# A spectral mixing layer and a state-space convolution in one kernel: the planner counts the wait for VectorE's own result, and the first tiles are split in another order

## The chip, the core and the metric

The kernel runs on one core of a Trainium2 chip. The metric is the device time of one execution in microseconds (us). A core has engines with instruction streams of their own: TensorE (PE in the profile; its weight loads are PEld), VectorE (DVE), ScalarE (ACT), GpSimd (POOL) and SyncE (SP, which here issues nearly all the transfers). They meet only at semaphores, and each runs its stream in the order in which it was written.

## The reference

Two independent parts, whose results stand side by side in the output:

```python
# A: x is (2048, 512); the four DFT matrices are inputs
a = x @ dft_hid_re.T;  b = x @ dft_hid_im.T
ya = dft_seq_re @ a - dft_seq_im @ b
# B: u is (2048, 512); A, C are (512, 128) complex; dt is (512,)
P = exp((A * dt)[:, :, None] * arange(2048))        # (512, 128, 2048)
K = 2 * real(einsum("dn,dnl->dl", C * dt, P))       # taps of a convolution, per channel
yb = irfft(rfft(u, 4096) * rfft(K, 4096))[:2048] + u * D_skip
out = concatenate([ya, yb])                          # (2048, 1024), float32
```

## The kernel before, in words

**Part A (class Fnet)** is dense matmul. Each float32 tile of 128x512 is split into a high and a low part: ScalarE copies it to `hi` (line 181), VectorE subtracts to get `lo` (line 183). One step of a product is then three matmuls, hi·hi, lo·hi and hi·lo (line 294), called a *triple* here; one moving tile feeds four triples. There are 12 groups (8 against x, 4 against the hidden-dimension matrix) and 640 triples in all. Three split moving tiles are held at once (`DEPTH`), four raw ones (`RAWS`).

**Part B (class Ssm)** makes the convolution's taps from tables of powers. The 512 channels go in 16 chunks of 32. For each chunk two tables grow by doubling, each step a product (`mul`, line 524, into `prod`) and the sum of its halves (`add`, line 533, into `t`): table 1 (`tables1`, 12 VectorE steps; two buffers `t1`) holds the coarse powers, table 2 (`tables2`, 19 steps; a single buffer `t2`) the fine ones, where even entries come from a squaring on ScalarE (lines 540, 547, 553). In `order`'s rows below both are called `t`: `t_124` is table 2, another number is table 1 of one chunk. A step of a table reads what the step ahead of it has written. When both tables of a chunk are done, TensorE makes the chunk's *taps* with 64 small matmuls (`taps`, line 720). They free both tables, so table 2 of the next chunk starts only after them. Then come an FFT as small matmuls (lines 793 for u, 750 for the taps, 871), the product of the spectra on VectorE (`product`, lines 887, 889, 897, 900) and the inverse (lines 907, 954). From the last chunk's taps on, no table work is left.

**What sets the order.** Nothing is moved by the compiler: `Plan` is a small list scheduler that runs when the program is written, and its choices become the order of every engine's stream. Each process is a generator; it yields the engine and an estimated duration, and waits for events and for counts of free buffers (`Sem`). Of the processes that are ready, the one that can start earliest is written next, and of those that can start equally early the one of lower urgency number (`key`, line 122). Where a process goes from one engine to another, `HOP` (0.3 us) is added to the time from which its next step is ready; between two steps on the same engine nothing is. Table 2 has urgency 2, table 1 2.2, part B's other work 1, and part A's matmuls 5, so that triples fill what part B leaves of TensorE. A tile's split has urgency 3 while three split tiles are ahead of TensorE, else 0.

**The start.** `load_x0` brings in the first 128 columns of x tile 0 and splits them, so that the first quarter of the first triples can begin; `load_x1` brings in the rest of tile 0 and the other x tiles; `load` the moving tiles, the first of them through ScalarE's queue. `warm` runs three matmuls on zeros ahead of them. A count `slots` of four raw x buffers holds the loads back.

Of the kernel before, what the change touches and what calls it, by code (L numbers as in the profile page):

```python
# [46 lines left out]
    return [np.ascontiguousarray(a.astype(np.float32)) for a in (f1u, f1k, w2, ia, ib)]  # L47


HOP, LATENCY = 0.3, 3.3  # L50
STREAM = 5


class Sem:
# [11 lines left out]
class Plan:  # L66
# [11 lines left out]
    def step(self, p, value):  # L78
        self.now = p[0]
        while True:  # L80
            try:
                r = p[3].send(value)
            except StopIteration:
                return
            value = None
            if isinstance(r, Event):
                if r.time is None:
                    r.waiting.append(p)
                    return
                p[0] = max(p[0], r.time)  # L90
            elif isinstance(r, Sem):
                if not r.free:
                    r.waiting.append(p)
                    return
                p[0] = max(p[0], r.free.pop(0))
            else:
                if r[0] != p[5]:
                    p[0] += HOP
                p[4], p[5] = r, r[0]
                self.ready.append(p)  # L100
                return
            self.now = p[0]
# [18 lines left out]

    def key(self, p):
        engine, _, *urgency = p[4]
        return max(p[0], self.free.get(engine, 0.0)), urgency[0]() if urgency else p[1], p[2]

    def run(self):

        while self.ready:
# [4 lines left out]
            if engine == "pe":  # L133
                stream = p[1] >= STREAM
                if stream != self.streaming:
# [7 lines left out]
def act(cols):  # L143
    return 0.09 + cols * 0.00085


def dve(cols, rate=1.0):
    return (62 + cols / rate) / 960


def load(kb):
    return max(0.55, kb / 330)


class Fnet:
# [36 lines left out]
    def warm(self):  # L192

        z, ps = self.pool.tile([128, DM], F32, name="y", bufs=STAGED), self.psum.tile([128, DM], F32, name="acc")
        yield "dve", 0.3
        self.nc.vector.memset(z, 0.0)
        yield "pe", 2.2
        for n in range(3):
            self.nc.tensor.matmul(ps[:, :216], z[:, :128], z[:, 256:472], start=n == 0, stop=n == 2)

    def still(self, k):
        return [self.pool.tile([128, DM], F32R, name=f"x_{m}{k}") for m in ("hi", "lo")]
# [17 lines left out]
                                     op=OP.subtract)  # L220
        self.plan.set(self.x0_ev)

    def load_x1(self, b, raw, n, slots):
        cols = slice(0 if n else 128, DM)
        yield "dma", load(256)
        self.nc.sync.dma_start(raw[:, cols], self.xin[n, :, cols])
        if n:
            self.x[n] = self.still(n)
        yield from self.split(*(a[:, cols] for a in self.x[n]), raw[:, cols])
        self.plan.put(slots)  # L230
        self.plan.set(self.x_ev[n])
        self.x_left -= 1
        if not self.x_left:
            self.plan.put(b.uks)

    def loads(self, b):
        yield b.uks
        x_raw = b.pool.tile([128, 4, DM], F32, name="uk", bufs=b.n)
        slots, self.x_left = Sem(4), 16
        for g in self.groups:  # L240
            for i in self.items[g]:
                urgency = -1 if i in self.items[self.groups[0]][:3] else 0
                if g == self.groups[0]:
                    yield slots
                    if not i[3]:
                        self.plan.spawn(self.load_x0(x_raw[:, 0]), -1)
                    self.plan.spawn(self.load_x1(b, x_raw[:, i[3] % 4], i[3], slots), urgency)
                if i[0] == "p":
                    k = i[1], i[3] // 4, i[3] % 4
                    yield self.p_ev[k]  # L250
                    src = self.p[k]
                else:
                    src = self.sT[i[1], i[2], i[3]]
                yield self.raws
                self.plan.spawn(self.load(src, None, self.m, i, self.m_ev[i]), urgency)
# [91 lines left out]
class Ssm:  # L347
# [118 lines left out]
    def params(self, par, alpha, dt):  # L466

        v = self.nc.vector
        n = par.shape[2]
        yield "dve", dve(n)  # L470
        v.tensor_tensor(par[:, 0], alpha, dt, op=OP.mult)
        yield "dve", dve(n)
        v.scalar_tensor_tensor(par[:, 1], par[:, 1], 1.0 / (2 * math.pi), dt, op0=OP.mult, op1=OP.mult)
        yield "dve", dve(n)
        v.tensor_tensor(par[:, 2], par[:, 2], dt, op=OP.mult)
        yield "dve", dve(n)
        v.scalar_tensor_tensor(par[:, 3], par[:, 3], -1.0, dt, op0=OP.mult, op1=OP.mult)

    def setup(self):
# [47 lines left out]
            seed.rearrange("p k d c -> p k (d c)")[:, :, :, None].to_broadcast([128, 2, 2 * nd, m]), op=OP.mult)  # L527
        return p

    def add(self, p, dst, rows):  # L530

        yield "dve", dve(2 * p.shape[2] * p.shape[4])
        self.nc.vector.tensor_tensor(dst[:, :, :, rows], p[:, 0], p[:, 1, :, ::-1], op=OP.add)  # L533

    def square(self, t, m, ev, box):
# [7 lines left out]

    def even_im(self, t, m):

        yield "dve", dve(t.shape[1] * m // 2)
        self.nc.vector.scalar_tensor_tensor(t[:, :, 1, m:2 * m:2], t[:, :, 0, m // 2:m], 2.0,  # L547
                                            t[:, :, 1, m // 2:m], op0=OP.mult, op1=OP.mult)

    def even_re(self, t, m, ev, box):  # L550
        yield ev
        yield "dve", dve(t.shape[1] * m // 2)
        self.nc.vector.tensor_tensor(t[:, :, 0, m:2 * m:2], box[0][:, :, 0], box[0][:, :, 1], op=OP.subtract)  # L553

    def seed_args(self, ck, box, ev):
# [99 lines left out]
    def tables2(self):  # L655
        a = self.nc.scalar
        for n in range(16):
            yield self.cs_ev[n]
            yield self.t2s
            cs, t = self.cs[n], self.t2  # L660
            yield "act", act(2 * CHUNK)
            a.activation(t[:, :, :, 1].rearrange("p d c -> p c d"), cs[:, :, 0, :, 0], AF.Copy)  # L662
            for c in range(2):
                yield "act", act(2 * CHUNK)
                a.activation(t[:, :, c, 2:6:2].rearrange("p d j -> p j d"), cs[:, c, 1:3, :, 0], AF.Copy)
            p = yield from self.mul("prod2", t, slice(1, 2), cs[:, :, 1])
            yield from self.add(p, t, slice(3, 4))
            p = yield from self.mul("prod2", t, slice(1, 4), cs[:, :, 2])
            yield from self.add(p, t, slice(5, 8))
            for m in (8, 16):  # L670
                ev, box = Event(), []
                self.plan.spawn(self.square(t, m, ev, box), 0)
                p = yield from self.mul("prod2", t, slice(1, m, 2), cs[:, :, 3 if m == 8 else 4])
                yield from self.even_im(t, m)
                yield from self.even_re(t, m, ev, box)
                yield from self.add(p, t, slice(m + 1, 2 * m, 2))
            yield from self.even_im(t, 32)
            for d in (slice(0, CHUNK // 2), slice(CHUNK // 2, CHUNK)):
                ev, box = Event(), []
                self.plan.spawn(self.square(t[:, d], 32, ev, box), 0)  # L680
                p = yield from self.mul("prod2", t[:, d], slice(1, 32, 2), cs[:, :, 5, d])
                yield from self.even_re(t[:, d], 32, ev, box)
                yield from self.add(p, t[:, d], slice(33, 64, 2))
            self.done_cs(n)
            self.plan.set(self.t2_ev[n])

# [173 lines left out]
    def product(self, b, h, q, got, done):  # L860
# [3 lines left out]
        for r in range(2):  # L864
            for n, name in enumerate("uk"):
                xt = self.xt[name, h, q]
                for c in range(2):
                    for xx in range(4):
                        for g in range(2):
                            rows, o = slice(64 * g, 64 * g + 64), (2 * n + c) * PART  # L870
                            nc.tensor.matmul(got[r][1][32 * xx:32 * xx + 32, g, o:o + PART],  # L871
                                             self.w2[rows, 2 * q + r, xx, 32 * c:32 * c + 32], xt[rows, r, xx],
                                             start=True, stop=True, tile_position=(64 * g, 32 * xx))
# [3 lines left out]
        u, t = uk[:, :, :, 0], uk[:, :, :, 1]  # L877
# [4 lines left out]
        def half(r, k, p):  # L882
            yield "act", act(1024)
            a.activation(uk[:, r].rearrange("p g n c d -> p g (n c d)"), p, AF.Copy)  # L884
            self.give(k)
            yield "dve", dve(512)
            v.tensor_tensor(P[:, r], t[:, r], u[:, r], op=OP.mult)  # L887
            yield "dve", dve(512)
            v.tensor_tensor(t[:, r], t[:, r], u[:, r, :, ::-1], op=OP.mult)  # L889
            left[0] -= 1  # L890
            if not left[0]:
                self.plan.set(ready)
        for r in range(2):
            self.plan.spawn(half(r, *got[r]), 1)
# [1 line left out]
        yield "dve", dve(512)  # L896
        v.tensor_tensor(u[:, :, :, 0], P[:, :, :, 0], P[:, :, :, 1], op=OP.subtract)
        self.plan.put(b.zbs)
        yield "dve", dve(512)
        v.tensor_tensor(t[:, :, :, 0], t[:, :, :, 0], t[:, :, :, 1], op=OP.add)  # L900

        def run(got):
# [16 lines left out]
        z = b.pool.tile([128, 2, 4, PART], F32, name="z", bufs=b.n)  # L919
# [132 lines left out]
```

## Time and profile before

| | |
|---|---|
| median of 3 runs | 618.55 us (618.45 to 620.91) |
| the profiled execution's own time | 619.57 us |
| its span, first to last instruction | 617.8 us |
| mean granted TensorE clock | 0.996 |
| busy in the span: TensorE, VectorE, ScalarE | 593.2, 511.1, 380.9 us |
| DMA: moved, mean rate | 125.97 MB, 204 GB/s |

The profile is one execution, 1.8 us of which lie outside the span; its own time is 1.0 us over the median. Matmul ends are modelled, and matmuls overlap, so a busy TensorE is not one at its peak; starts of matmuls are safe to compare. A row of the timeline reads: start, duration, engine, line, operation, output<-input, shapes, and in brackets the idle time ahead of it with what ended that.

### The profile page before, as it was taken

The numbers are of one execution on the slowest core, as the hardware profiler recorded it, in microseconds if no ns is written. First come the engines' busy times: TensorE is split into PE (matmuls) and PEld (weight loads), VectorE is DVE, ScalarE is ACT, GpSimd is POOL, SyncE is SP. The second block draws the span as 40 slices with busy tenths as digits, with TensorE's granted clock in tenths as the row PEclk, the third lists the DMA queues.
The fourth block names the chain that finished last, engine by engine and source line by source line (L and its number), as shares of the span: only waits on it lengthen the run. The fifth ranks groups of instructions, "written<-read, shape, count | busy, mean of one in ns | idle before, by whom it ended". The sixth has DMA issues, their size and how long they took to land.

```text
span 617.8 us, 16971 instructions
## 1 busy us (share of the span) xinstructions
PE 593.2 (96%) x6982; PEld 451.4 (73%) x6982; DVE 511.1 (83%) x883; ACT 380.9 (62%) x745; POOL 3.6 (1%) x12
## 2 busy tenths in 40 slices
PE   8999999999999998999999999999999899999997
PEld 6875766777778776868777777777777677777775
DVE  6999989999999999999999999999999742535120
ACT  5769978544674778754869555774865345455332
POOL 0000000000000000000000000000000000000000
PEclk9999999999999999999999999999999899999999
DMA  8989985832574557346858565567968548996761
GB/s 279 288 319 324 329 266 173 248 120 75 145 219 125 154 150 213 110 136 181 276 179 234 142 187 143 156 180 242 256 180 251 166 126 236 349 275 197 255 206 69
DMA packets 141150, 125.97 MB, mean 204 GB/s; under 512 B 46224, under 2 KB 106128, under 8 KB 140816
## 3 DMA queue, kind: packets, MB, share of 16 engines
q1 hardware_dynamic: 140656, 124.49, 67.2%
q8 instruction: 55, 0.90, 0.6%
q10 hardware_dynamic: 416, 0.39, 0.2%
q14 instruction: 23, 0.19, 0.1%
HBM read 82.12 MB, written 42.73 MB: 202 GB/s over the span
## 4 chain that ended last, share of the span: by engine, by line
DVE 39%; PE 35%; issue 10%; DMA 8%; ACT 5%; SPq 1%; DVEq 0%; ACTq 0%
PE acc L294 26%; DVE prod L524 10%; DVE t L533 8%; DVE lo L183 8%; PE f L871 3%; DMA zl<-zs 2%; DVE t L553 2%; PE f L954 2%; PE f L720 2%; PE f L907 2%; DVE z L887 1%; DVE x_lo L183 1%; DVE t L547 1%; DVE cs L594 1%; DVE uk L889 1%
## 5 line engine op out<-in xcount | busy, mean ns | idle before, releaser
L294 PE MATMUL acc<-hi,x_hi 128*128 128x512 f32 x640 | 259.0, 405 | 3.7 <-ACT y L308 2.4
L294 PE MATMUL acc<-lo,x_hi 128*128 128x512 f32 x640 | 252.9, 395 | 7.8 <-DVE lo L183 7.6
L294 PE MATMUL acc<-hi,x_lo 128*128 128x512 f32 x640 | 251.0, 392 | 0.0
L524 DVE TENSOR_TENSOR prod<-t,cs 128x1024 f32<-128x1024 f32 (+3 forms) x192 | 167.2, 872 | 7.9 <-ACT t L662 2.3
L183 DVE TENSOR_TENSOR lo<-raw,hi 128x512 fp32r<-128x512 f32 x160 | 109.6, 687 | 68.5 <-ACT hi L181 59.0
L294 PEld LDWEIGHTS acc<-hi,x_hi 128*128 128x128 f32 x640 | 120.8, 189 | 51.0 <-issue 18.9
L294 PEld LDWEIGHTS acc<-lo,x_hi 128*128 128x128 f32 x640 | 120.9, 189 | 37.0 <-DVE lo L183 14.2
L294 PEld LDWEIGHTS acc<-hi,x_lo 128*128 128x128 f32 x640 | 121.0, 189 | 25.8
L181 ACT ACTIVATE hi<-raw 128x512 fp32r<-128x512 f32 x160 | 100.4, 629 | 62.9 <-PE acc L294 54.0
L533 DVE TENSOR_TENSOR t<-prod 128x512 f32<-128x512 f32 (+4 forms) x192 | 98.5, 515 | 3.5
L540 ACT ACTIVATE square<-t 128x256 f32<-128x256 f32 (+1 forms) x64 | 36.8, 575 | 43.9 <-DVE t L533 35.3
L308 ACT ACTIVATE y<-acc 128x512 f32<-128x512 f32 x48 | 28.7, 600 | 22.4 <-PE acc L294 19.9
L720 PEld LDWEIGHTS f<-t,t 128*32 128x32 f32 x2048 | 29.5, 110 | 8.6 <-issue 5.0
L884 ACT ACTIVATE uk<-f 128x1024 f32<-128x1024 f32 x32 | 31.7, 1017 | 6.5 <-PE f L871 6.5
L720 PE MATMUL f<-t,t 128*32 128x64 f32 x2048 | 32.6, 220 | 2.0 <-DVE t L533 1.3
L887 DVE TENSOR_TENSOR z<-uk 128x512 f32<-128x512 f32 x32 | 22.0, 687 | 7.6 <-ACT uk L884 6.2
L922 ACT ACTIVATE z<-f 128x512 f32<-128x512 f32 x32 | 17.7, 595 | 14.8 <-PE f L907 7.5
L553 DVE TENSOR_TENSOR t<-square 128x128 f32<-128x128 f32 (+1 forms) x64 | 24.8, 387 | 0.0
L871 PE MATMUL f<-xt_k,w 64*32 64x128 f32 x1024 | 22.9, 271 | 1.0 <-issue 1.0
L889 DVE TENSOR_TENSOR uk<-uk 128x512 f32<-128x512 f32 x32 | 22.1, 690 | 0.7
L547 DVE SCALAR_TENSOR_TENSOR t<-t 128x128 f32<-128x128 f32 (+2 forms) x48 | 22.3, 466 | 0.2
L599 ACT ACTIVATE cs<-cs 128x352 f32<-128x352 f32 x32 | 16.0, 533 | 10.0 <-DVE cs L594 10.0
(85 smaller groups left out, 442.2 us busy)
## 6 DMA issues: line engine op xcount, KB each, us to landing
raw<-in_sT SPq DMA_DIRECT2D x127, 256.0 KB, 3.1
p<-y SPq DMA_DIRECT2D x32, 256.0 KB, 3.8
xt_u<-xu SPq DMA_DIRECT2D x32, 256.0 KB, 4.7
xk<-xk_sb SPq DMA_DIRECT2D x32, 256.0 KB, 4.0
xt_k<-xk SPq DMA_DIRECT2D x32, 256.0 KB, 5.3
zs<-z SPq DMA_DIRECT2D x32, 256.0 KB, 3.5
zl<-zs SPq DMA_DIRECT2D x16, 512.0 KB, 6.3
raw<-p SPq DMA_DIRECT2D x32, 256.0 KB, 4.0
```

The costliest lines, as they stand in the source:

```text
L181: self.nc.scalar.activation(hi, src, AF.Copy)
L183: self.nc.vector.tensor_tensor(lo, src, hi.bitcast(F32), op=OP.subtract)
L294: nc.tensor.matmul(acc[d], l[:, cols], r, start=k == 0 and n == 0, stop=k == len(items) - 1 and n == 2)
L308: self.nc.scalar.activation(y, ps, AF.Copy, scale=-1.0 if g[2] == 1 else 1.0)
L524: self.nc.vector.tensor_tensor(p.rearrange("p k d c m -> p k (d c) m"), src.rearrange("p d c l -> p (d c) l")[:, None, :, rows].to_broadca ...
L533: self.nc.vector.tensor_tensor(dst[:, :, :, rows], p[:, 0], p[:, 1, :, ::-1], op=OP.add)
L540: self.nc.scalar.activation(sq, t[:, :, :, m // 2:m], AF.Square)
L547: self.nc.vector.scalar_tensor_tensor(t[:, :, 1, m:2 * m:2], t[:, :, 0, m // 2:m], 2.0, t[:, :, 1, m // 2:m], op0=OP.mult, op1=OP.mult)
L553: self.nc.vector.tensor_tensor(t[:, :, 0, m:2 * m:2], box[0][:, :, 0], box[0][:, :, 1], op=OP.subtract)
L720: nc.tensor.matmul(ps[32 * j:32 * j + 32, i], t1[:, d, c], t2[:, d, c], start=c == 0, stop=c == 1, tile_position=(0, 32 * j))
L871: nc.tensor.matmul(got[r][1][32 * xx:32 * xx + 32, g, o:o + PART], self.w2[rows, 2 * q + r, xx, 32 * c:32 * c + 32], xt[rows, r, xx], star ...
L884: a.activation(uk[:, r].rearrange("p g n c d -> p g (n c d)"), p, AF.Copy)
```

## The change

A step on VectorE that follows another VectorE step of the same process, and whose yield has no third value, becomes ready `RESULT` = 0.15 us after the one ahead has ended, in the plan. Steps that are marked with `APART` (third value None, fourth True) are exempt: they read nothing that the step just ahead in their process wrote, or it is old enough. Since the plan then has one table's next step ready 0.15 us late, another process's step is written in between. Three other edits concern the start: the rest of x tile 0 is split only after the first moving tile's split is planned; the count `slots` gives way to a wait for the split of the x tile four before; the three matmuls of `warm` have 256 columns instead of 216, with a planned time of 2.6 us.

```diff
-HOP, LATENCY = 0.3, 3.3
+HOP, RESULT, LATENCY = 0.3, 0.15, 3.3
+APART = None, True
...
                 if r[0] != p[5]:
                     p[0] += HOP
+                elif r[0] == "dve" and len(r) < 4:
+                    p[0] += RESULT
...
-        return max(p[0], self.free.get(engine, 0.0)), urgency[0]() if urgency else p[1], p[2]
+        return max(p[0], self.free.get(engine, 0.0)), urgency[0]() if urgency and urgency[0] else p[1], p[2]
...
-        yield "pe", 2.2
+        yield "pe", 2.6
         for n in range(3):
-            self.nc.tensor.matmul(ps[:, :216], z[:, :128], z[:, 256:472], start=n == 0, stop=n == 2)
+            self.nc.tensor.matmul(ps[:, :256], z[:, :128], z[:, 256:], start=n == 0, stop=n == 2)
...
         if n:
             self.x[n] = self.still(n)
+        else:
+            yield self.m_ev[self.items[self.groups[0]][0]]
         yield from self.split(*(a[:, cols] for a in self.x[n]), raw[:, cols])
-        self.plan.put(slots)
...
-                    yield slots
+                    if i[3] >= 4:
+                        yield self.x_ev[i[3] - 4]
...
-    def add(self, p, dst, rows):
-
-        yield "dve", dve(2 * p.shape[2] * p.shape[4])
+    def add(self, p, dst, rows, *apart):
+
+        yield "dve", dve(2 * p.shape[2] * p.shape[4]), *apart
...
     def even_im(self, t, m):
 
-        yield "dve", dve(t.shape[1] * m // 2)
+        yield "dve", dve(t.shape[1] * m // 2), *APART
...
-                yield from self.add(p, t, slice(m + 1, 2 * m, 2))
+                yield from self.add(p, t, slice(m + 1, 2 * m, 2), *APART)
...
-            yield "dve", dve(512)
+            yield "dve", dve(512), *APART
             v.tensor_tensor(t[:, r], t[:, r], u[:, r, :, ::-1], op=OP.mult)
```

The four steps of `params`, `even_re`, the last `add` of table 2 and the last step of `product` are marked with `APART` in the same way.

**VectorE, in the middle of the tables, before.** `t_2358` is table 1 of one chunk, `t_124` is table 2:

```order
L524 TENSOR_TENSOR prod<-t_2358,cs 128x128
L533 TENSOR_TENSOR t_2358<-prod 128x64
L524 TENSOR_TENSOR prod<-t_2358,cs 128x256
L533 TENSOR_TENSOR t_2358<-prod 128x64x2
L524 TENSOR_TENSOR prod<-t_2358,cs 128x512
L533 TENSOR_TENSOR t_2358<-prod 128x64x4
L524 TENSOR_TENSOR prod<-t_2358,cs 128x1024
L533 TENSOR_TENSOR t_2358<-prod 128x64x8
```

One table runs alone, each row needing the row ahead of it. The same steps of the next chunk now (`t_2275` is table 1; lines 524 and 533 have become 529 and 538):

```order
L529 TENSOR_TENSOR prod_2287<-t_124,cs 128x128
L529 TENSOR_TENSOR prod<-t_2275,cs 128x128
L538 TENSOR_TENSOR t_124<-prod_2287 128x64
L538 TENSOR_TENSOR t_2275<-prod 128x64
L529 TENSOR_TENSOR prod_2311<-t_124,cs 128x384
L529 TENSOR_TENSOR prod<-t_2275,cs 128x256
L538 TENSOR_TENSOR t_124<-prod_2311 128x64x3
L186 TENSOR_TENSOR lo<-raw,hi 128x512
```

The two tables alternate, and no row needs the one just ahead. Counted over VectorE's whole stream, 295 of its instructions wait for the VectorE instruction just ahead of them before, and 135 now.

**ScalarE, at the start, before** (`x_hi_140` is x tile 0, `x_hi_150` x tile 1, `hi` a moving tile):

```order
L217 ACTIVATE x_hi_140<-uk 128x128
L181 ACTIVATE x_hi_140<-uk 128x384
L181 ACTIVATE hi<-raw 128x512
L181 ACTIVATE x_hi_150<-uk 128x512
L181 ACTIVATE hi<-raw 128x512
```

and now (lines 217 and 181 have become 220 and 184):

```order
L220 ACTIVATE x_hi_140<-uk 128x128
L184 ACTIVATE hi<-raw 128x512
L184 ACTIVATE x_hi_150<-uk 128x512
L184 ACTIVATE hi<-raw 128x512
L184 ACTIVATE x_hi_140<-uk 128x384
```

The rest of x tile 0 has moved behind the first two moving tiles and x tile 1.

**SP's queue, some ten transfers in, now** (`raw` is a moving tile, `uk` an x tile):

```order
L270 DMA raw<-in_sT 128x512
L394 DMA f1u<-in_f1u 128x128
L394 DMA f1k<-in_f1k 128x256
L394 DMA dskip<-in_dsk 128x128
L229 DMA uk<-in_x 128x512
```

Part B's three constants, which stood some 20 rows further back, are now ahead of the fifth x tile; u's spectrum (line 793) starts after 34 triples instead of 55.

More of the change, by code (lines that the diff above doesn't have):

```diff
@@ L221, in load_x0, with load_x1 @@
         self.plan.set(self.x0_ev)
-    def load_x1(self, b, raw, n, slots):
+    def load_x1(self, b, raw, n):
         cols = slice(0 if n else 128, DM)
@@ L238, in loads @@
         x_raw = b.pool.tile([128, 4, DM], F32, name="uk", bufs=b.n)
-        slots, self.x_left = Sem(4), 16
+        self.x_left = 16
         for g in self.groups:
@@ L243, in loads @@
                 if g == self.groups[0]:
-                    yield slots
+                    if i[3] >= 4:
+                        yield self.x_ev[i[3] - 4]
                     if not i[3]:
                         self.plan.spawn(self.load_x0(x_raw[:, 0]), -1)
-                    self.plan.spawn(self.load_x1(b, x_raw[:, i[3] % 4], i[3], slots), urgency)
+                    self.plan.spawn(self.load_x1(b, x_raw[:, i[3] % 4], i[3]), urgency)
                 if i[0] == "p":
@@ L469, in params @@
         n = par.shape[2]
-        yield "dve", dve(n)
+        yield "dve", dve(n), *APART
         v.tensor_tensor(par[:, 0], alpha, dt, op=OP.mult)
-        yield "dve", dve(n)
+        yield "dve", dve(n), *APART
         v.scalar_tensor_tensor(par[:, 1], par[:, 1], 1.0 / (2 * math.pi), dt, op0=OP.mult, op1=OP.mult)
-        yield "dve", dve(n)
+        yield "dve", dve(n), *APART
         v.tensor_tensor(par[:, 2], par[:, 2], dt, op=OP.mult)
-        yield "dve", dve(n)
+        yield "dve", dve(n), *APART
         v.scalar_tensor_tensor(par[:, 3], par[:, 3], -1.0, dt, op0=OP.mult, op1=OP.mult)
@@ L551, in even_re @@
         yield ev
-        yield "dve", dve(t.shape[1] * m // 2)
+        yield "dve", dve(t.shape[1] * m // 2), *APART
         self.nc.vector.tensor_tensor(t[:, :, 0, m:2 * m:2], box[0][:, :, 0], box[0][:, :, 1], op=OP.subtract)
@@ L682, in tables2 @@
                 yield from self.even_re(t[:, d], 32, ev, box)
-                yield from self.add(p, t[:, d], slice(33, 64, 2))
+                yield from self.add(p, t[:, d], slice(33, 64, 2), *APART)
             self.done_cs(n)
@@ L898, in product @@
         self.plan.put(b.zbs)
-        yield "dve", dve(512)
+        yield "dve", dve(512), *APART
         v.tensor_tensor(t[:, :, :, 0], t[:, :, :, 0], t[:, :, :, 1], op=OP.add)
```

## The prediction

> **What bounds the kernel now.** The page comes first: busy totals, VectorE's line of the 40 slices, and the chain that ended last.
>
> ```profile
> PE 593.2 (96%) x6982; PEld 451.4 (73%) x6982; DVE 511.1 (83%) x883; ACT 380.9 (62%) x745; POOL 3.6 (1%) x12
> DVE  6999989999999999999999999999999742535120
> DVE 39%; PE 35%; issue 10%; DMA 8%; ACT 5%; SPq 1%; DVEq 0%; ACTq 0%
> ```
>
> Two engines look full, so shares don't decide. VectorE's line does: it is full to about slice 31 (485 us) and then drops. There are two stages, with the last chunk's taps as the border. The timeline of TensorE gives the taps of chunks 0, 1 and 15 (line 720), and the price of matmuls:
>
> ```profile
> 71.77 0.39 PE L294 MATMUL acc<-hi,x_lo 128*128 128x512 f32 x1
> ...
> 72.45 0.39 PE L294 MATMUL acc<-hi,x_lo 128*128 128x512 f32 x1
> 72.77 1.44 PE L720 MATMUL f<-t,t 128*32 128x64 f32 x88
> ...
> 99.19 1.99 PE L720 MATMUL f<-t,t 128*32 128x64 f32 x128
> 101.12 0.50 PE L294 MATMUL acc<-hi,x_hi 128*128 128x512 f32 x1
> 101.45 0.39 PE L294 MATMUL acc<-lo,x_hi 128*128 128x512 f32 x1
> ...
> 493.61 1.99 PE L720 MATMUL f<-t,t 128*32 128x64 f32 x128
> ```
>
> Three matmul starts take 72.45 - 71.77 = 0.68 us: a triple. Chunks 1 to 15 take 493.61 - 99.19 = 394.4 us, and 617.8 - 493.6 = 124.2 us follow. Busy time by stretch (columns: length, then PE, PEld, DVE, ACT, POOL):
>
> ```profile
> 99.20:493.70 394.50, 379.34 (x5023) 291.82 (x5026) 381.21 (x651) 252.99 (x506) 3.15 (x7) 1.00 0.62 177
> ...
> 560.00:600.00 40.00, 40.00 (x391) 30.84 (x390) 11.93 (x18) 16.72 (x28) 0.00 (x0) 1.00 0.74 225
> ```
>
> In the last stage TensorE is full and VectorE half idle: TensorE is the bound there. In the table stage the waits, by engine over 40 to 490 us, tell who is late:
>
> ```profile
> DVE prod L524 <- ACT t L662: 2.3, 2, 2.0
> ...
> PE acc L294 <- DVE lo L183: 7.6, 9, 1.8
> PE acc L294 <- ACT y L308: 2.0, 4, 0.7
> ```
>
> VectorE waits for almost nothing; TensorE waits mostly for VectorE's `lo`. What VectorE's 13.3 us without busy time consist of is seen in its timeline:
>
> ```profile
> 347.99 1.23 DVE L524 TENSOR_TENSOR prod<-t,cs 128x1024 f32<-128x1024 f32 x1
> 349.25 0.69 DVE L533 TENSOR_TENSOR t<-prod 128x512 f32<-128x512 f32 x1
> 349.98 1.22 DVE L524 TENSOR_TENSOR prod<-t,cs 128x1024 f32<-128x1024 f32 x1
> 351.23 0.69 DVE L533 TENSOR_TENSOR t<-prod 128x512 f32<-128x512 f32 x1
> 351.84 0.68 DVE L183 TENSOR_TENSOR lo<-raw,hi 128x512 fp32r<-128x512 f32 x1
> 352.44 0.37 DVE L524 TENSOR_TENSOR prod<-t,cs 128x128 f32<-128x128 f32 x1
> ```
>
> An instruction that needs the one ahead starts 0.03 to 0.04 us after its end (349.25, 349.98, 351.23). One that doesn't starts 0.08 us before it (351.84, 352.44). Over all neighbours 277 gaps are of the first kind (0.035) and 544 of the second (-0.084); a dependent pair costs 0.119 us. In the stage 233 instructions depend: 233 x 0.035 = 8.2 us of the 13.3, so VectorE is filled to 98.7% (381.2 + 8.2 of 394.5). TensorE's own work there, from the chain's rows:
>
> ```profile
> 173.25 1.96 PE f L871 x128
> 492.63 1.05 PE f L907 x32
> 493.68 1.92 PE f L720 x128
> 507.56 1.93 PE f L750 x16
> 541.33 1.90 PE f L954 x32
> ```
>
> is 408 triples x 0.681 = 277.8, 14 taps x 1.92, 11 products x 1.96, 11 inverses x 1.05, 7 x 1.93 and 4 x 1.90, in all 359; with 0.1 us lost on entering and on leaving each of some 36 such pieces (101.12 to 101.45 is 0.33 instead of 0.23), 366. TensorE has 28 us to spare, VectorE 5: VectorE is the bound of the table stage. One late split even costs twice, since TensorE restarts at half pace (0.43 instead of 0.23 between starts):
>
> ```profile
> 484.64 0.40 PE L294 MATMUL acc<-hi,x_hi 128*128 128x512 f32 x1
> 486.86 0.71 PE L294 MATMUL acc<-lo,x_hi 128*128 128x512 f32 x1 [1.82 <-DVE lo L183]
> 487.36 0.63 PE L294 MATMUL acc<-hi,x_lo 128*128 128x512 f32 x1
> 487.79 0.63 PE L294 MATMUL acc<-hi,x_hi 128*128 128x512 f32 x1
> ```
>
> **The change part by part.** *Alternation.* Counted along VectorE's stream up to the last step of the last table: 821 instructions with 285 dependent pairs before, 826 with 123 now. The five more are splits:
>
> ```profile
> L183 DVE TENSOR_TENSOR lo<-raw,hi 128x512 fp32r<-128x512 f32 x160 | 109.6, 687 | 68.5 <-ACT hi L181 59.0 <-DMA out_ya<-y 9.3
> ```
>
> So VectorE saves 162 x 0.119 = 19.3 us and takes on 5 x (0.687 - 0.084) = 3.0. From chunk 1 to 15 its stream is 138 pairs, 16.4 us, shorter (657 instructions for 659): 389.4 plus 5 of waits become 378.
>
> The Trainium skill speaks against this term: "VectorE: DVE Perf Modes", The DRAIN you can't avoid, says that the next operation doesn't start until the pipe is empty, and that a semaphore after each of eight copies cost nothing. By it the term is 0. The trace disagrees, with 544 starts 0.084 us ahead of the end and 277 behind it.
>
> *TensorE's order.* 529 triples now stand ahead of the last taps instead of 511, with the same pieces of part B. The last stage is 18 x 0.681 = 12.3 us shorter: 111.9 us. It still has 100 triples between the last taps and the last inverse (101 before), so its cover is unchanged; the closing run of triples falls from 28 to 11, 7.5 us, which still covers the last output's copy and store.
>
> *First taps.* 88 triples stand ahead of chunk 0's taps instead of 80, and 111 instead of 103 ahead of chunk 1's. TensorE is the one that sets that time: 99.2 + 8 x 0.681 = 104.6. VectorE comes with chunk 1 at 99 to 103, since table 2's single buffer is freed only by the later taps of chunk 0.
>
> *Table stage together.* TensorE from chunk 1 to 15: 418 triples now, so 366 + 10 x 0.681 = 373, from 104.6 to 477.6. VectorE: 101 + 378 = 479. They are within 1%; the later one counts, 479. With the last stage, 479 + 111.9 = 590.9 us of span.
>
> *What two full engines lose to each other.* From below 0. From above the waits for something other than `lo`, some 8 us of rows as the ACT row above, that VectorE's lateness covers now. I take 4, the middle, since both ends are of the same kind.
>
> *The start.* ScalarE and TensorE before:
>
> ```profile
> 4.25 0.52 ACT L181 ACTIVATE x_hi<-uk 128x384 fp32r<-128x384 f32 x1 [0.48 <-DMA uk<-in_x]
> 4.68 0.61 ACT L181 ACTIVATE hi<-raw 128x512 fp32r<-128x512 f32 x1
> 5.93 0.63 ACT L181 ACTIVATE hi<-raw 128x512 fp32r<-128x512 f32 x1
> ...
> 5.35 0.79 PE L294 MATMUL acc<-hi,x_hi 128*128 128x512 f32 x1 [1.24 <-ACT hi L181]
> ...
> 7.09 0.63 PE L294 MATMUL acc<-hi,x_hi 128*128 128x512 f32 x1
> ...
> 9.18 0.40 PE L294 MATMUL acc<-hi,x_lo 128*128 128x512 f32 x1
> ```
>
> The first moving tile can be split 0.4 to 0.9 us earlier, so the first triple starts at about 4.5. But the second triple needs the rest of x tile 0, now behind the second moving tile, whose copy began at 5.93: 5.93 + 0.63 + 0.52 = 7.1, as before (7.09). Pace was half until 9.18; half pace may end up to 4 us earlier or 2 us later, worth -2 to +1; I take 0, as the second triple's time stands. The wider warm matmuls end about where the first triple now starts: 0. The new wait in place of `slots` holds the same four buffers: 0.
>
> *Transfers moved forward.* Three constants (256 KB) pass an x tile in SP's queue, and u's spectrum (eight pieces of 512 KB in and 1 MB out) starts 21 triples earlier, while x tiles still load. The last column is GB/s; the third row is an issue, its time until landing last:
>
> ```profile
> 0.00:40.00 40.00, 37.18 (x150) 30.15 (x151) 33.53 (x74) 23.29 (x46) 0.20 (x4) 1.00 0.91 303
> 40.00:80.00 40.00, 38.28 (x279) 25.14 (x278) 38.96 (x67) 38.85 (x81) 0.00 (x0) 1.00 0.90 303
> ...
> xt_u<-in_uG SPq DMA_DIRECT2D x4, 512.0 KB, 4.5
> ```
>
> Counted along SP's queue, 8.5 MB stand up to the first piece's input and 23.3 MB up to the eighth's; at 303 GB/s they are moved by 28 and 77 us, and TensorE, by its own work, comes to them at about 32 and 81. With 4.5 us from issue to landing nothing is left over: 0 if all goes by the mean rate, 4 if each of the eight pieces waits half a microsecond. I take 1.
>
> Sum: 590.9 + 4 + 0 + 1 = 595.9 us of span. The profile's span lies 0.75 us below the median of the runs (617.8 and 618.55; the execution itself took 619.57): **597 us**.
>
> **The rivals.** (1) *Handovers eat half.* Table 2 has one buffer; now that both engines are full, each of 14 handovers from taps to table 2 and back could cost 1 us: 609 us. For it: the ACT t row, up to 2.0 us at one. Against: 2.3 us in total. (2) *Dependent pairs cost nothing to remove*, as the gaps could be a way of recording. Then VectorE only takes on 3.0 and the last stage gives 12.3: 609 us. Against: with these gaps the stream fills its stage to 98.7%. The Trainium skill's section above amounts to this rival. (3) *It does nothing measurable*: VectorE ends early, but the early transfers and ScalarE hold TensorE for as long, 616 to 621 us. Against: ScalarE is busy 253 of 394.5 us. (4) *Slower.* Table 2 lies between two taps; stretched by table 1's steps in between, it could make every taps wait. In the new stream it takes 14 to 22 us of VectorE from first to last step, between taps 16 to 29 us apart: about 4 us of room. It decides from 4 + 21.5 / 15 = 5.4 us of stretch a chunk; at 6, 597 + 15 x 2 = 627 us. Against: the planner gives table 2 the lower number.
>
> **How the numbers follow.** Half a per cent, 3 us, is what a measurement here tells from no change. Forecast 0.73, (1) 0.11, (2) 0.04, (3) 0.07, (4) 0.05. Faster 0.88, same 0.07, slower 0.05. Low end: TensorE alone, 477.6 + 111.9, with 2 us from the start: 588. High end: 8 for the losses, 4 for transfers and 1 for the pace give 605; to 610 to take in (2) and half of (1).
>
> The Trainium skill ("TensorE: Matmul & The Clock Gate", Part 1) lets full pace come after some 3.4 us of work and go after an idle window of that length. Here a 1.8 us wait was enough (486.86), so that stalls left over may cost more than it says.
>
> **What would show it.** Right: dependent gaps about 120; chunk 1's taps at 103 to 107 us, chunk 15's at 478 to 486; TensorE's waits for `lo` mostly gone; 110 to 114 us after the last taps. Wrong: gaps between alternating steps that stay positive (2); VectorE waiting for ScalarE's copies into table 2, over 5 us (1, 4); TensorE starved by transfers before 60 us (3).

## The result, and the profile after

The changed kernel takes 596.00 us (median of 6 runs, 594.21 to 597.86), beside 619.79 us for the kernel before in the same series (618.45 to 621.17): a ratio of 0.9619 [0.9594, 0.9643]. The profiled execution took 596.03 us, its span 594.2 us, 23.6 us less than the span before. (Executions with a granted TensorE clock held down throughout, to 0.85 in the one that occurred, are left out of the comparisons below.)

The page first: busy totals, VectorE's 40 slices, and the chain that ended last.

```profile
PE 583.7 (98%) x6982; PEld 451.0 (76%) x6982; DVE 496.2 (84%) x883; ACT 380.7 (64%) x745; POOL 4.7 (1%) x12
DVE  6985989999999999999999999999999954255410
PE 82%; DVE 7%; ACT 6%; issue 2%; DMA 2%; SPq 0%; ACTq 0%; DVEq 0%
```

VectorE holds the last chain for 7% instead of 39%, TensorE for 82% instead of 35%. VectorE's work is as many instructions as before (883), and 14.9 us less of busy time. Its line now stays full to about 475 us (slice 32 of 594.2 us) and then drops.

The timeline of TensorE at the taps of chunks 1 and 15 (now line 725), and the busy time of the two stages that they bound:

```profile
103.71 1.99 PE L725 MATMUL f<-t,t 128*32 128x64 f32 x128
...
483.07 1.97 PE L725 MATMUL f<-t,t 128*32 128x64 f32 x122
```

```profile
103.70:483.10 379.40, 376.74 (x5051) 296.35 (x5051) 372.47 (x657) 256.57 (x514) 4.28 (x7) 1.00 0.63 183
483.10:594.20 111.10, 106.39 (x1412) 82.49 (x1405) 37.30 (x56) 47.61 (x76) 0.24 (x1) 0.99 0.73 224
```

So the 23.6 us are: chunk 1's taps 4.5 us later (99.2 to 103.7), the table stage 15.0 shorter (394.4 to 379.4) although it holds ten more triples, and the last stage 13.1 shorter (124.2 to 111.1).

VectorE's timeline in an alternating stretch, and two rows where a pair still depends:

```profile
249.90 1.55 DVE L529 TENSOR_TENSOR prod<-t,cs 128x256 f32<-128x256 f32 x2
251.37 0.28 DVE L538 TENSOR_TENSOR t<-prod 128x128 f32<-128x128 f32 x1
251.57 0.68 DVE L186 TENSOR_TENSOR lo<-raw,hi 128x512 fp32r<-128x512 f32 x1
252.17 0.42 DVE L558 TENSOR_TENSOR t<-square 128x256 f32<-128x256 f32 x1
252.50 0.68 DVE L538 TENSOR_TENSOR t<-prod 128x512 f32<-128x512 f32 x1
...
288.05 1.23 DVE L529 TENSOR_TENSOR prod<-t,cs 128x1024 f32<-128x1024 f32 x1
289.31 0.69 DVE L538 TENSOR_TENSOR t<-prod 128x512 f32<-128x512 f32 x1
```

The first five follow each other 0.08 us before the end of the one ahead (249.90 + 1.55 = 251.45, and the next starts at 251.37). At 289.31 a sum waits for its own product and starts 0.03 us after the end, as before. Over the whole trace the gaps of the second kind (a start 0 to 0.06 us after the end) have fallen from 277 to 130, those of the first (a start ahead of the end) risen from 544 to 700.

The page's groups for the triple's second matmul and the split that it needs, the last column being idle time ahead and what ended it:

```profile
L299 PE MATMUL acc<-lo,x_hi 128*128 128x512 f32 x640 | 250.5, 391 | 0.1
L186 DVE TENSOR_TENSOR lo<-raw,hi 128x512 fp32r<-128x512 f32 x160 | 109.1, 686 | 63.9 <-ACT hi L184 63.9
```

TensorE's 7.6 us of waits for `lo` are gone. TensorE executes as many matmuls as before (6982), and its time without busy work falls from 24.6 us (617.8 - 593.2) to 10.5 (594.2 - 583.7). Counted by starts, which also takes in matmuls at half pace, the delays of 0.15 us or more against the usual step fall by about 20 us (an estimate; it hangs by a us or two on what is taken as usual). So most of the 23.6 us are stalls of TensorE that are gone.

### The profile page after: what moved, and what is told of

Read it like the earlier page. It is cut to its first block, busy times and chain, and to the rows that moved or that the text cites. A ratio compares the mean times of both kernels' runs of the same rounds, so it can differ in the third digit from the quotient of the medians.

```text
span 594.2 us, 16953 instructions
## 1 busy us (share of the span) xinstructions
PE 583.7 (98%) x6982; PEld 451.0 (76%) x6982; DVE 496.2 (84%) x883; ACT 380.7 (64%) x745; POOL 4.7 (1%) x12
## 4 chain that ended last, share of the span: by engine, by line
PE 82%; DVE 7%; ACT 6%; issue 2%; DMA 2%; SPq 0%; ACTq 0%; DVEq 0%
PE acc L299 64%; PE f L876 5%; PE f L725 5%; PE f L912 3%; PE f L959 3%; DVE prod L529 2%; PE f L755 2%; DVE lo L186 2%; DVE t L538 2%; ACT hi L184 1%; DMA uk<-in_x 1%; ACT L586 1%; DMA raw<-in_sT 1%; DMA xu<-z 1%; ACT seed L574 1%
## 5 line engine op out<-in xcount | busy, mean ns | idle before, releaser
L529 DVE TENSOR_TENSOR prod<-t,cs 128x1024 f32<-128x1024 f32 (+4 forms) x192 | 163.3, 869 | 3.6 <-ACT t L667 1.4
L538 DVE TENSOR_TENSOR t<-prod 128x512 f32<-128x512 f32 (+4 forms) x192 | 94.4, 511 | 1.1
L558 DVE TENSOR_TENSOR t<-square 128x128 f32<-128x128 f32 (+1 forms) x64 | 24.6, 384 | 0.3 <-ACT square L545 0.3
L552 DVE SCALAR_TENSOR_TENSOR t<-t 128x128 f32<-128x128 f32 (+2 forms) x48 | 22.3, 465 | 0.4
```

Source lines behind the costliest of these rows:

```text
L529: self.nc.vector.tensor_tensor(p.rearrange("p k d c m -> p k (d c) m"), src.rearrange("p d c l -> p (d c) l")[:, None, :, rows].to_broadca ...
```

## Experiments

Each kernel was timed beside the kernel before on the same chip (medians of the kernel before: 620.82, 620.03 and 619.70 us in the three series). The first four kernels split the change: alternation, the wait counted in the plan, and the start. The first two have the changed kernel's start, so their ratios to the kernel before hold what that start costs.

**Wait counted, no alternation** (charged). The 0.12 us are put on VectorE's own time, so that no other step is drawn in between.

```diff
-HOP, RESULT, LATENCY = 0.3, 0.15, 3.3
+HOP, RESULT, LATENCY = 0.3, 0.12, 3.3
...
-                    p[0] += RESULT
+                    r = (r[0], r[1] + RESULT, *r[2:])
```

> The plan charges the wait for the own result to VectorE itself (0.12 us longer) instead of making the step ready later: the time is counted, but the tables don't alternate (288 dependent pairs up to the last table, 285 before). 576 triples stand ahead of the last taps, 64 behind. If any plan that knows VectorE's true time and fills TensorE with triples does it: chunk 1's taps at 104 us, chunk 15's at 510, table stage bound by TensorE (405 us of work against VectorE's 401), then 78 us if 64 triples cover the last stage (590 us), up to 100 if they don't (612). If the dependent pairs themselves must go: no gain, 617 to 621 us.

Measured: 614.5 us, ratio 0.9885 [0.9855, 0.9915]; 281 dependent gaps. Chunk 15's taps come at 518.0 and the last stage takes 95.6 us. Windows of the table stage and of the end, and a row of the waits from 495 us on (us in total, times, longest):

```profile
103.00:518.00 415.00, 409.15 (x5188) 323.57 (x5187) 395.38 (x674) 268.90 (x534) 3.82 (x7) 1.00 0.62 179
...
580.00:600.00 20.00, 12.49 (x246) 8.55 (x244) 7.47 (x12) 7.89 (x13) 0.00 (x0) 0.83 0.49 148
600.00:613.60 13.60, 5.54 (x64) 5.33 (x64) 0.42 (x1) 2.17 (x4) 0.00 (x0) 0.74 0.73 233
```

```profile
PE f L959 <- DMA zl<-zs: 8.6, 1, 8.6
```

TensorE is without work for 15.6 of its last 33.6 us (33.6 - 12.49 - 5.54), 8.6 of them in one wait for a transfer, at a granted clock of 0.74 to 0.83. With true times the plan does fill the table stage with triples: 576 stand ahead of the last taps, and TensorE has 409 us of work in the stage's 415. So the last taps come 24 us later than before, and the 64 triples that are left don't cover part B's end. The time lies between the two that were expected (up to 612 us, or 617 to 621). Counting the wait alone is worth 1.1%, well short of the change.

**Alternation, wait hardly counted** (barely_later).

```diff
-HOP, RESULT, LATENCY = 0.3, 0.15, 3.3
+HOP, RESULT, LATENCY = 0.3, 0.001, 3.3
```

> RESULT is 0.001 us instead of 0.15: the tables alternate (119 dependent pairs up to the last table), but the plan hardly counts the wait; 510 triples stand ahead of the last taps, as before (511). If the removed pairs shorten VectorE's stage as predicted: chunk 1's taps at 102 us, chunk 15's at 475 to 480, then 125 us: 600 to 606 us. If the gain is all in the plan's true times: 615 to 620 us.

Measured: 602.77 us, ratio 0.969 [0.9656, 0.9724]; 128 dependent gaps; taps of chunks 1 and 15 at 101.1 and 473.2. Windows of its two stages:

```profile
101.10:473.20 372.10, 367.18 (x5002) 287.50 (x5001) 367.71 (x651) 253.96 (x508) 4.80 (x7) 1.00 0.64 182
...
473.20:598.30 125.10, 120.27 (x1470) 93.01 (x1462) 41.38 (x62) 52.22 (x83) 0.24 (x1) 1.00 0.71 217
```

A thousandth of a microsecond is enough to make the tables alternate, and the table stage shrinks by 22.3 us to 372.1, of which VectorE has 4.4 us without busy time, where it had 13.3. But the plan, which had never counted the wait, goes on handing out as many triples as before (510 ahead of the last taps), and the last stage keeps its length (124.2 before). So alternation brings the larger part, 3.1%. Counting the wait moves 19 triples forward (529 instead of 510), and the changed kernel is a further 0.7% faster; that step is no larger than what re-planned versions differ by further down, so its size isn't shown.

**Tables without the start** (tables_only): the alternation as in the change, and `load_x1`, `loads` and `warm` as before.

```diff
-        yield "pe", 2.6
+        yield "pe", 2.2
...
-        else:
-            yield self.m_ev[self.items[self.groups[0]][0]]
...
-                    if i[3] >= 4:
-                        yield self.x_ev[i[3] - 4]
+                    yield slots
```

> The alternation alone, with the start of before. VectorE 374 us and TensorE 370 us from chunk 1's taps to chunk 15's, 122 triples behind them. If the start's edits cost about 1.5 us of TensorE (half pace until 12.3 instead of 9.1 us): 593 to 597 us. If the start's edits help: 598 to 600 us.

Measured: 598.6 us, ratio 0.9609 [0.9562, 0.9655], beside 0.9619 [0.9594, 0.9643] with the start. (The plain quotient of the medians is 0.964, which lies in the interval too.) Inconclusive: the two can't be told apart, also because the plan comes out differently further on (518 triples ahead of the last taps instead of 529, and waits of 2.2 us at 311 and 2.6 us at 535 that the changed kernel doesn't have).

**The start without the tables** (start_only).

```diff
-HOP, RESULT, LATENCY = 0.3, 0.15, 3.3
+HOP, RESULT, LATENCY = 0.3, 0.0, 3.3
```

> The start's edits alone, RESULT 0. 305 dependent pairs up to the last table. VectorE-bound as before: 2.3 us more of VectorE up to the last table, and 131 triples behind it instead of 129: 620 to 624 us. If the start's edits help by themselves: 615 to 618 us.

Measured: 625.1 us, ratio 1.007 [1.0048, 1.0091]. On their own the start's edits lose 3.0 to 5.6 us. TensorE's timeline there:

```profile
7.72 0.80 PE L299 MATMUL acc<-hi,x_hi 128*128 128x512 f32 x1 [1.43 <-ACT x_hi L184]
8.31 0.63 PE L299 MATMUL acc<-lo,x_hi 128*128 128x512 f32 x1
...
13.43 0.49 PE L299 MATMUL acc<-lo,x_hi 128*128 128x512 f32 x1
13.77 0.40 PE L299 MATMUL acc<-hi,x_lo 128*128 128x512 f32 x1
```

The second triple starts 0.6 us later than before (7.09), behind a wait for the rest of x tile 0, and full pace comes at 13.4 us instead of 9.2. But the whole loss isn't there: chunk 1's taps come at 98.0 us, with five triples fewer ahead of them than before, the table stage takes 398.4 us instead of 394.4, with 20 dependent gaps more in the trace (297 instead of 277), and the last stage 127.4 instead of 124.2, with 131 triples instead of 129. How much of the 3.0 to 5.6 us is the start and how much the altered plan stays open.

Start_only is also the fairest measure for alternation. It differs from barely_later in `RESULT` alone (0 instead of 0.001), and was timed in the same series: 625.1 against 602.77 us, ratios of 1.007 and 0.969. With the same start in both, alternation is worth 22 us.

**What a dependent pair costs** (pairs). Behind the changed kernel's work stand series of additions on three small tiles: each on the same tile (`pa`, line 994), alternating between two (line 997), and a read of a tile followed by a write to it (lines 999 and 1000), 32 and 128 columns wide.

```diff
+    for n in (32, 128):
+        for _ in range(16):
+            v.tensor_tensor(x[:, :n], x[:, :n], z[:, :n], op=OP.add)
+        for _ in range(8):
+            for t in (x, y):
+                v.tensor_tensor(t[:, :n], t[:, :n], z[:, :n], op=OP.add)
+    for _ in range(8):
+        v.tensor_tensor(x, y, z, op=OP.add)
+        v.tensor_tensor(y, z, z, op=OP.add)
```

> The changed kernel with short VectorE series at its end: 16 additions in place on one tile (each needs the one ahead), 16 that alternate between two tiles (each needs the one before the last), at 32 and at 128 columns; then 8 pairs of which the second overwrites what the first reads. If a dependent pair costs 0.119 us whatever its size: 1.9 us between the two series of 16 at both sizes. If waiting for the own result costs nothing: 0.

VectorE's timeline at the end of the span (one row can hold several instructions, xcount):

```profile
583.91 3.59 DVE L994 TENSOR_TENSOR pa<-pa,pc 128x32 f32<-128x32 f32 x16
587.53 0.19 DVE L997 TENSOR_TENSOR pa<-pa,pc 128x32 f32<-128x32 f32 x1
...
589.34 5.19 DVE L994 TENSOR_TENSOR pa<-pa,pc 128x128 f32<-128x128 f32 x16
594.56 0.29 DVE L997 TENSOR_TENSOR pa<-pa,pc 128x128 f32<-128x128 f32 x1
594.77 0.28 DVE L997 TENSOR_TENSOR pb<-pb,pc 128x128 f32<-128x128 f32 x1
...
597.60 0.28 DVE L997 TENSOR_TENSOR pb<-pb,pc 128x128 f32<-128x128 f32 x1
597.92 0.29 DVE L999 TENSOR_TENSOR pa<-pb,pc 128x128 f32<-128x128 f32 x1
598.24 0.29 DVE L1000 TENSOR_TENSOR pb<-pc 128x128 f32<-128x128 f32 x1
598.57 0.29 DVE L999 TENSOR_TENSOR pa<-pb,pc 128x128 f32<-128x128 f32 x1
```

With 32 columns sixteen dependent additions take 587.53 - 583.91 = 3.62 us, 0.226 each; sixteen alternating ones 589.34 - 587.53 = 1.81, 0.113 each. With 128 columns it is 0.326 (594.56 - 589.34 = 5.22 for sixteen) and 0.203 (597.60 - 594.56 = 3.04 for fifteen). A pair costs 0.11 to 0.12 us at both widths, by starts alone. A write to a tile that the one ahead reads (598.24) comes 0.32 us after it, the same as a read of what was written (598.57, 0.33). This settles rival 2: the gaps are time, and no way of recording. (It is one execution.) The Trainium skill ("VectorE: DVE Perf Modes", The DRAIN you can't avoid) says that the next op doesn't start until the pipe is empty, and adds that one that isn't held starts earlier. The prediction took the first half alone, by which its term would be 0; the independent additions, which started early, agree with the second half.

**Which engine bounds which kernel** (before_less_dve, before_less_dve2, after_less_dve). VectorE is given 22 us less work in the whole kernel and the plan is left as it was, by leaving out one step of the spectra's product.

```diff
-            v.tensor_tensor(t[:, r], t[:, r], u[:, r, :, ::-1], op=OP.mult)
```

> The kernel before, with line 889 (one of the four VectorE products of the spectra, 32 instructions) left out of the stream but not of the plan, so that every other instruction stands where it stood; the result of part B is then wrong. Up to the last table VectorE has 22 instructions and 15.4 us less. If VectorE bounds the table stage before: chunk 15's taps 15 us earlier, 602 to 605 us. If TensorE does: 615 to 619 us.

> The changed kernel with the same line left out (894 there): 14.9 us less of VectorE up to the last table, 362 us against TensorE's 373 from chunk 1 to 15. If TensorE bounds it now: 590 to 596 us, no more than 6 us gained. If VectorE still does: 581 to 584 us.

> before_less_dve once more, for its trace, with the same text: VectorE bounds the table stage before and has 15.4 us less, so that chunk 15's taps come 15 us earlier if nothing else is near; TensorE's own work (366 us against VectorE's 378) is now within 3%, and what two nearly full engines lose to each other, 4 to 6 us in the changed kernel, may be lost here too: 9 to 15 us earlier, 603 to 610 us.

Measured: the kernel before, 606.87 and 610.4 us, ratio 0.9812 [0.9765, 0.986], and again, 609.21 us, 0.9832 [0.9804, 0.986]: less was gained than the 602 to 605 us first expected, and the second expectation (603 to 610) was met. The changed kernel, 595.51 us, 0.9595 [0.9561, 0.9629], is 0.0024 or 1.5 us below its ratio with the step, inside the interval. The table stages, of the kernel before and then of the changed one, both with less VectorE work:

```profile
100.20:482.00 381.80, 374.47 (x5020) 291.12 (x5020) 367.37 (x629) 252.93 (x506) 4.08 (x7) 1.00 0.63 182
```

```profile
103.00:481.50 378.50, 375.52 (x5050) 296.53 (x5049) 361.20 (x635) 256.84 (x514) 4.37 (x7) 1.00 0.64 183
```

Before, 22 instructions and 13.8 us less on VectorE between the taps (381.2 to 367.4) shorten the stage by 12.6 us: VectorE was its bound, and with 374.5 of 381.8 us busy TensorE is then close behind. After, 11.3 us less (372.5 to 361.2) shorten it by 0.9, and TensorE is busy for 375.5 of the 378.5 us: TensorE is the bound now.

**A better start, tried** (tile0_second). In the changed kernel's plan x tiles 1 and 2 and the moving tiles behind the first are held back until the rest of x tile 0 is split, so that the second triple needn't wait (the first cut is in `load_x1`, the second in `load`).

```diff
+        if n in (1, 2):
+            yield self.x_ev[0]
...
+        if key in self.items[self.groups[0]][1:3]:
+            yield self.x_ev[0]
```

> The changed kernel, but the rest of x tile 0 is split right after the first moving tile (x tiles 1 and 2 and moving tiles 1 and 2 wait for it in the plan). The second triple starts at 5.8 to 6.0 us instead of 7.5, TensorE doesn't idle and keeps full pace from 5.5 us on: at 13 us it is 16 matmuls ahead, 3.7 us. If TensorE bounds the whole kernel now: 591 to 594 us. If VectorE holds the table stage: 595 to 597 us.

Measured: 599.34 us, ratio 0.9661 [0.9624, 0.9699]: not better than the change, and above both times that were expected (591 to 594 and 595 to 597 us). TensorE's timeline at the start, and late:

```profile
5.92 0.39 PE L303 MATMUL acc<-hi,x_hi 128*128 128x512 f32 x1
...
540.39 0.66 PE L880 MATMUL f<-xt_k,w 64*32 64x128 f32 x29 [1.96 <-issue]
...
541.73 0.63 PE L303 MATMUL acc<-hi,x_lo 128*128 128x512 f32 x1
```

The start does what it was meant to: the second triple begins at 5.92, full pace stays, and at 13 us some 16 matmuls more have started than in the changed kernel. But the plan came out otherwise to the end: 525 triples stand ahead of the last taps instead of 529, and single waits stand in it, at 461 (2.3 us) and at 540 (2.0, with 3.4 us of half pace behind it). The lead of some 3.5 us is gone at the end; these waits account for most of that, as far as the trace tells.

**Later transfers on top** (second_late4, second_late5). The same kernel, with the plan expecting a transfer's data 4.0 and 5.0 us after its issue instead of 3.3; and the changed kernel once more beside them (changed_again).

```diff
-HOP, RESULT, LATENCY = 0.3, 0.15, 3.3
+HOP, RESULT, LATENCY = 0.3, 0.15, 4.0
```

> tile0_second with the plan's time until a transfer has landed raised from 3.3 to 4.0 us (the issues' rows show 3.0 to 6.3). The new plan gives VectorE 11 to 15 us of lead at every chunk's taps, where tile0_second had 5 to 10, and 538 triples ahead of the last taps. If TensorE's late restarts of tile0_second came from a plan that believed transfers faster than they are: few stalls over 0.4 us after 40 us, start 3.7 us ahead, 589 to 594 us. If any plan within a few us loses about as much somewhere: 595 to 600 us.

> The same with 5.0 us. 28 triples between the last spectrum of the taps and the next product's matmuls (26 in tile0_second), 23 ahead of the last inverses (18), 521 triples ahead of the last taps. If longer cover in the last stage is what tile0_second lacked: no stall over 1 us after 490 us, 590 to 595 us. If not: 596 to 601 us.

> The changed kernel once more, beside the versions of this call: 594 to 598 us, 0.959 to 0.965 of before.

Measured: 599.5 us, 0.9679 [0.9653, 0.9706]; 603.77 us, 0.9743 [0.9716, 0.9769]; and 596.12 us, 0.9624 [0.9604, 0.9645] for the change, as expected. The first bears out its second alternative (595 to 600 us), the second lies above both of its own. With 5.0 the waits in the last stage are gone, and new ones come up earlier:

```profile
21.00 0.49 PE L303 MATMUL acc<-hi,x_hi 128*128 128x512 f32 x1 [4.46 <-ACT hi L184]
...
467.19 0.41 PE L880 MATMUL f<-xt_k,w 64*32 64x128 f32 x4 [3.08 <-issue]
...
468.09 0.40 PE L303 MATMUL acc<-hi,x_lo 128*128 128x512 f32 x1
```

No version tried is shown to beat the changed kernel. Versions that all alternate lie at 596 to 604 us. What seems to decide between them is where a few waits of 1.5 to 4.5 us fall, since each edit of the plan moves them; that is read from one trace of each and not shown, and the executions of one version also differ, by up to 6.5 us (596.46 to 603.00 in tile0_second). I can't say beforehand where such waits fall.

## Why the prediction came out as it did

*VectorE as the bound of the table stage before*: shown, by before_less_dve2 (12.6 of 13.8 us came back).

*162 pairs at 0.119 us*: the price is shown by pairs (0.113 and 0.12). The trace has 147 dependent gaps fewer (277 to 130), the stream of instructions some 160; the rest presumably wait for something else last. Between the taps of chunks 1 and 15 the trace has 122 gaps fewer (209 to 87) where the prediction took 138, so the saving there is 14.5 us by this price and not 16.4. The additional splits are seen in part: VectorE's count in the stage went from 651 to 657 instructions, three of them splits (102 to 105), where the prediction had 659 and 657.

*The 12.3 us of triples moved forward*: the last stage measured 111.1 us, 111.9 were forecast. Barely_later shows it from the other side, with 510 triples ahead and 125.1 us. The cover held: the last stage lost nothing new.

*Table stage*: chunk 15's taps at 483.1, where the terms gave 479 + 4 = 483. But the working named VectorE as the later engine, 479 against TensorE's 477.6, and after_less_dve shows that it is TensorE: with VectorE relieved the stage still takes 378.5 us, 5.5 more than the 373 that I counted for TensorE. So the 4 us were not what two full engines lose to each other; most stay with one of them relieved. They are TensorE's time without work, 2.7 us of the stage (379.4 - 376.74), and what my count of its pieces missed. By the same measure TensorE needed 371.7 us of the stage before (378.5 - 10 x 0.681), so that it had an estimated 23 us to spare there and not 28; VectorE was the bound all the same. The number came out because both engines were within 1.4 us of each other, and because a term put in for another reason stood where TensorE's missing time belongs. In that it was luck.

*The start at nothing*: in the profiled execution it cost more than the term allowed. Rows of TensorE and of ScalarE in the changed kernel:

```profile
4.38 0.79 PE L299 MATMUL acc<-hi,x_hi 128*128 128x512 f32 x1
...
7.47 0.49 PE L299 MATMUL acc<-hi,x_hi 128*128 128x512 f32 x1 [1.49 <-ACT x_hi L184]
...
9.18 0.63 PE L299 MATMUL acc<-hi,x_lo 128*128 128x512 f32 x1
...
12.46 0.39 PE L299 MATMUL acc<-lo,x_hi 128*128 128x512 f32 x1
```

```profile
5.72 0.63 ACT L184 ACTIVATE x_hi<-uk 128x512 fp32r<-128x512 f32 x1 [1.39 <-DMA uk<-in_x]
6.37 0.63 ACT L184 ACTIVATE hi<-raw 128x512 fp32r<-128x512 f32 x1
6.91 1.03 ACT L184 ACTIVATE x_hi<-uk 128x384 fp32r<-128x384 f32 x2
```

The first triple came at 4.38 as forecast (4.5), the second at 7.47 (7.1): I had counted the second moving tile ahead of the rest of x tile 0, at its time before (5.93), but not x tile 1, which the new order also puts there and which ScalarE waited 1.39 us for. Then half pace lasted from 8.9 to 12.3 us, where before it ended at 9.2. At 13 us 19 matmuls of the triples had started, where 25 had before: 6 x 0.227 = 1.4 us, above the term's upper end of 1. But how long half pace lasts at the start differs between executions of the same start. The 31st of these matmuls starts at 14.2 us in the kernel before and at 14.8 in before_less_dve2; with the new start it comes at 15.7 here, at 14.8 in changed_again and at 15.0 in after_less_dve. So the start costs between nothing and 1.5 us. It didn't show at chunk 1's taps: waits from 40 to 100 us that TensorE had had before (1.7 us) were gone, and these taps came at 103.7 where 104.6 was forecast (at 104.65 in changed_again).

*Transfers at 1 us*: no loss seen. From 40 to 80 us, where u's spectrum now stands, TensorE is full at 339 GB/s, more than the 303 that I had taken as the rate:

```profile
40.00:80.00 40.00, 40.00 (x170) 27.16 (x169) 31.34 (x59) 37.45 (x82) 0.00 (x0) 1.00 0.97 339
```

*The rivals.* (1) was put at 609 us, but 14 handovers at 1 us on top of 597 make 611. (1) and (4) would show as waits for table 2; from 40 to 490 us there is one of 1.4 us:

```profile
DVE prod L529 <- ACT t L667: 1.4, 1, 1.4
```

(2) fell with pairs. (3) fell with the taps, which came 10.5 us earlier.

What stays open: whether the start's edits cost anything in the changed kernel, since tables_only and the change have overlapping intervals; and why a re-planned version falls where it does within 596 to 604 us.

## What to carry to other kernels

Where one engine runs a chain in which each step needs the last, look at the gap between the end of one instruction and the start of the next: if it is positive there and negative elsewhere, a second, independent chain written in between gets the difference back for each step. It may help further if a planner that places other work by such times counts the wait too: alternating alone gave 3.1%, counting alone 1.1%, both 3.8%, each with the new start. And before speeding up an engine that looks like the bound, work out what the next engine needs in that stage: here, with the pairs gone, 11 us less of VectorE's work shortened the stage by 1.

## What was not expected of the hardware

TensorE's pace is not told by the length of a wait. Behind waits of 1.49 us (7.47 in the changed kernel), 1.82 (486.86 before) and 1.96 (540.39 in tile0_second) it fell to half, for 3.4 us each time in the granted clock (8.88 to 12.29, 486.98 to 490.39, 541.34 to 544.75); behind one of 3.08 us (467.19 in second_late5) it didn't, the matmuls at 468.09 lasting 0.40 us, nor behind one of 2.27 us (460.75 in tile0_second). In changed_again the same start never had full pace before 9.9 us and didn't lose it afterwards. The Trainium skill ("TensorE: Matmul & The Clock Gate", Part 1) has a window of about 3.4 us that runs freely, and the length of the slow stretches agrees with it; that half pace needs an idle window of that length doesn't agree with waits of 1.5 to 2 us.

The price of a dependent pair on VectorE hardly grows with the width (0.113 us at 32 columns, 0.12 at 128), and is paid as well when the second instruction only overwrites what the first one reads (0.32 us from start to start at 128 columns, beside 0.203 without dependence).
